# The first transfer of `p` moved from SyncE's transfer queue to ScalarE's, in a fused attention and token-mixing kernel

## The chip, the cores and the metric

The kernel runs on one core of one Trainium2 chip. A core has a matrix engine (TensorE, PE in the profile), three engines for element-wise work (VectorE, DVE; ScalarE, ACT; GpSimd, POOL) and SyncE (SP), which does no arithmetic. Each engine works through its own instruction list in order and waits on semaphores where it needs another's result. Data come from and go to device memory (HBM) through 16 DMA engines, which the five instruction lists feed: a transfer issued by SP or ACT stands in the profile as `hardware_dynamic`, one issued by POOL as `software_dynamic`. The metric is the device time of the kernel in microseconds; lower is better.

## The reference

Two attention steps and a token-mixing step, over a batch of 8, with 8 heads, 576 tokens and 64 channels a head; `p` holds 32 packing queries for each head. Cut to what matters:

```python
p_packed = sm_attn(p, k, v)               # softmax(p k^T / 8) v : 32 x 64 for each head
out = sm_attn(q, p_packed, p_packed)      # softmax(q p_packed^T / 8) p_packed : 576 x 64 for each head
x = out.transpose(0, 2, 1, 3).reshape(8, 576, 512)
wq, wk = x @ w_q, x @ w_k                 # 576 x 64
W_tok = einsum('bsd,btd->bst', wq, wk) / 8
mixed = einsum('bst,btd->bsd', W_tok, x)
result = maximum(mixed, 0) @ w_out        # float32, 8 x 576 x 512
```

## The kernel before

The work is cut by batch element; the 8 batches run as a software pipeline, so that stages of several batches stand interleaved. The order is written out by hand: one string, `SCHEDULE`, lists some 600 small operations as `name@batch`, then a letter for the engine that copies a result (`s` ScalarE, `v` VectorE, `g` GpSimd) and the accumulator banks. A loop at the end of the kernel (L796 to L802) emits them in that order. Each engine's instruction list is what this string gives that engine, and no scheduler changes it.

For one batch: `k` (transposed per head by TensorE, `kt`, and copied to `kT`, `ke`) meets `p` in `s0` (L345); `nm0`, `ex0` and `ex1` make the exponentials; `xt` transposes them; `pv` (L421) multiplies by `v`; `pp`, `pt`, `pq` give the packed values and their products with the weights; `q` is transposed (`qt`), scored against the packed values (`e0` to `e2`, L470 and L482), and the later names up to `o0` to `o4` (L755) are the mixing and the last product, whose results SyncE stores.

Loads. Most go out on GpSimd's queue, because they turn float32 in HBM into bfloat16 on chip: `LK`, `LQ`, `LV` (`load`, L146 to L155) bring a whole batch of `k`, `q` or `v`, 576 KB as written on chip and twice that as read. `PB` (L178) brings all of `p` in bfloat16, `cw0` to `cw3` and `wo0`, `wo1` the weights. Batch 0 is treated apart, so that the pipeline fills sooner:

- `PF` (L164 to L166) loads `p` of batch 0 in float32 into `p_f`, 64 KB; `pfc@0s` (L213) casts it to `p_h` on ScalarE; `tp` (L217) transposes it on TensorE, and `lp` copies it to `pT_bd`, which `s0` reads.
- `KB` and `KA` (`first_k`, L168) load `k` of batch 0 in float32 on SyncE's queue in two halves of 576 KB, `kf[1]` first. `cB0`, `cB1`, `cA0` (VectorE) and `cA1` (ScalarE) cast them to `k_sb` (L247); `kf2`, `kf3` transpose the half of `KB`, `kf0`, `kf1` that of `KA` (L252), and `kfe0` to `kfe3` copy the results to `kT`.
- `w1` and `w2` (L200) are matrix products of a zero tile, with no use for the result.

The start of the order reads:

```python
SCHEDULE = """
    w1@0c:6 LQ@0 PF@0 pfc@0s KB@0 cw3@0 w1@0f:1 cB1@0v w1@0f:2 w2@0f:1 cw0@0 PB@0 LV@0 cB0@0v LK@1
    w1@0c:2 LK@2 KA@0 id@0 w1@0f:2 cA1@0s w1@0c:6 LQ@1 w2@0c:1 w1@0c:6 w2@0f:0 w1@0c:7 tp@0:0
    kf3@0:1 w1@0f:5 kf2@0:5 w1@0c:3 LV@1 cA0@0v kfe3@0v kf1@0:7 cw2@0 kf0@0:4 lp@0v w1@0f:6 w1@0c:0
```

Read by engine, SyncE's list begins `PF`, `KB`, `KA`, and its next entry is a store of results. GpSimd's begins `LQ@0`, `cw3`, `cw0`, `PB`, `LV@0`, `LK@1`, `LK@2`, `id` (the identity matrix for the transposes), `LQ@1`, `LV@1`. ScalarE's begins with the load of its function table, then `pfc`, `cA1`. The ninth transfer of GpSimd's list, `LV@1`, waits for the first to land, and so on.

Of the kernel before, what the change touches and what calls it, by code (L numbers as in the profile page):

```python
# [68 lines left out]
def kernel(  # L69
# [12 lines left out]
    nc = tc.nc  # L82
# [77 lines left out]
    p_f = sbp.tile([P, 2, Dh], fp32, name="p_f")  # L160
# [2 lines left out]

    @op  # L164
    def PF(b):
        nc.sync.dma_start(p_f, p[0].rearrange("(g x) l d -> (x l) g d", g=2))  # L166

    def first_k(gp, b):  # L168
        nc.sync.dma_start(
# [663 lines left out]
```

## Time and profile before

| | us |
|---|---|
| median of 3 runs | 119.72 |
| lowest, highest | 119.58, 120.13 |
| the profiled execution's own time | 119.49 |
| its span, first to last instruction | 117.7 |

| engine | busy us | share of the span |
|---|---|---|
| TensorE, products | 105.6 | 90% |
| VectorE | 91.1 | 77% |
| ScalarE | 88.0 | 75% |
| GpSimd | 60.1 | 51% |

The profile is of one execution, whose time is 0.23 us under the median of the runs; what lies outside its span is 119.49 - 117.7 = 1.8 us. Times within it are counted from the span's start. In the rows, `SPq` and `POOLq` (or POOL with `DMA_DIRECT2D`) are the issuing of a transfer; a row's brackets give the idle time of the engine before it and what ended it. `x20` is the number of instructions merged into a row, and rows of one engine may overlap. GB/s counts the bytes as written, so a load that halves the width reads twice its figure. A DMA share is a sum of the times of packets over 16 engines; as packets of one engine overlap, it can be over 1.

### The profile page before, as it was taken

How to read it: one execution, taken by the hardware profiler on the slowest of the kernel's cores; microseconds unless marked ns; L12 is line 12 of the kernel's file. 1: busy time of each engine (PE TensorE's matmuls, PEld its weight loads, DVE VectorE, ACT ScalarE, POOL GpSimd, SP SyncE). 2: the span in 40 equal slices, each digit the busy share in tenths (PEclk: the TensorE clock that was granted, in tenths of full speed). 3: DMA queues.
4: the chain of work that ended last, by engine and by line, in shares of the span. 5: the costliest groups of instructions: out<-in, count | busy, mean ns of one | idle time of the engine just before them, and what ended most of it. 6: DMA issues, size and time to landing. Idle time of an engine off the chain costs nothing.

```text
span 117.7 us, 4778 instructions
## 1 busy us (share of the span) xinstructions
PE 105.6 (90%) x2065; PEld 68.6 (58%) x2081; DVE 91.1 (77%) x184; ACT 88.0 (75%) x164; POOL 60.1 (51%) x88
## 2 busy tenths in 40 slices
PE   5997587887988999999999999999999999999950
PEld 1234456575855857778665875867566566545520
DVE  5326958999989989999999999698999967571420
ACT  5005574699879899899589999999898967678430
POOL 6965342278558994645981283606697780000000
PEclk9999999999999999999999999999999999999997
DMA  3999999999999999999999999999932174464793
GB/s 41 291 269 198 213 202 207 208 198 208 208 208 206 207 207 209 209 207 208 251 249 207 207 207 282 220 205 362 354 138 89 57 305 166 199 267 184 288 369 145
DMA packets 17925, 25.47 MB, mean 216 GB/s; under 512 B 2160, under 2 KB 14448, under 8 KB 17904
## 3 DMA queue, kind: packets, MB, share of 16 engines
q0 software_dynamic: 13920, 14.49, 73.2%
q1 hardware_dynamic: 3984, 10.68, 24.0%
q8 instruction: 16, 0.26, 0.8%
q14 instruction: 5, 0.04, 0.1%
HBM read 30.21 MB, written 9.44 MB: 337 GB/s over the span
## 4 chain that ended last, share of the span: by engine, by line
PE 63%; DMA 23%; DVE 7%; issue 2%; POOL 2%; ACT 1%; DVEq 0%; POOLq 0%
PE psum L755 27%; DMA k_sb<-in_k_dram 16%; PE psum L304 8%; DMA q_sb<-in_q_dram 7%; PE psum L421 3%; PE psum L714 3%; PE psum L571 3%; PE psum L660 3%; PE psum L376 3%; PE psum L628 2%; PE psum L470 2%; PE psum L345 2%; PE psum L683 1%; DVE nmax L355 1%; DVE kT L141 1%
## 5 line engine op out<-in xcount | busy, mean ns | idle before, releaser
L755 PE MATMUL psum<-w_out,r 128*64 128x512 bf16 (+1 forms) x208 | 30.9, 380 | 0.6 <-issue 0.3
L551 POOL TENSOR_TENSOR a<-e,rr 128x512 bf16<-128x512 f32 (+1 forms) x19 | 16.6, 891 | 7.2 <-ACT e L135 2.5
L755 PEld LDWEIGHTS <-r 128*64 128x64 bf16 (+1 forms) x216 | 12.3, 108 | 10.2 <-issue 1.1
L135 ACT ACTIVATE o_sb<-psum 128x512 f32<-128x512 f32 x24 | 14.5, 609 | 4.2 <-PE psum L755 4.2
L135 ACT ACTIVATE r<-psum 128x512 bf16<-128x512 f32 x24 | 13.3, 603 | 1.9 <-PE psum L714 1.9
L203 PE MATMUL psum<-zero 128*64 128x512 bf16 (+1 forms) x43 | 11.9, 487 | 2.5 <-DVE zero L182 1.2
L498 DVE TENSOR_REDUCE mx<-psum 128x16 f32<-128x512 f32 (+1 forms) x24 | 12.5, 551 | 1.8 <-PE psum L470 1.6
L359 ACT ACTIVATE e1T<-psum,nmax 128x576 bf16<-128x576 f32 x16 | 11.8, 740 | 2.8 <-DVE nmax L355 2.6
L502 DVE TENSOR_TENSOR e<-psum,mx 128x512 f32<-128x512 f32 (+1 forms) x24 | 12.4, 549 | 0.3
L540 POOL TENSOR_TENSOR rt<-e 128x576 f32<-128x576 f32 x5 | 7.1, 1422 | 10.3 <-ACT e L531 10.3
L355 DVE TENSOR_REDUCE nmax<-psum 128x2 f32<-128x1152 f32 x8 | 10.8, 1354 | 0.9 <-PE psum L345 0.8
L304 PE MATMUL psum<-ident,q_sb 128*64 128x128 bf16 x288 | 10.2, 220 | 0.4 <-DMA q_sb<-in_q_dram 0.4
L531 ACT ACTIVATE e<-e 128x1152 f32<-128x1152 f32 x8 | 9.3, 1164 | 1.0 <-DVE e L502 1.0
L135 ACT ACTIVATE kT<-psum 128x1280 bf16<-128x1280 bf16 (+3 forms) x8 | 8.0, 1013 | 2.3 <-PE psum L304 2.3
L304 PEld LDWEIGHTS <-q_sb 128*64 128x64 bf16 x288 | 8.6, 110 | 1.0 <-DMA q_sb<-in_q_dram 0.5
L304 PE MATMUL psum<-ident,k_sb 128*64 128x128 bf16 x252 | 9.0, 220 | 0.1
L141 DVE COPY o_sb<-psum 128x512 f32<-128x512 f32 x8 | 5.5, 685 | 4.0 <-PE psum L755 3.8
L542 POOL TENSOR_TENSOR rt<-rt 128x288 f32<-128x288 f32 (+2 forms) x15 | 7.9, 527 | 1.2
L148 POOL DMA_DIRECT2D v_sb<-in_v_dram x8 | 6.2, 779 | 4.3 <-DMA q_sb<-in_q_dram 2.4
L304 PEld LDWEIGHTS <-k_sb 128*64 128x64 bf16 x252 | 7.8, 110 | 0.9 <-issue 0.2
L203 PEld LDWEIGHTS <-zero 128*64 128x64 bf16 (+1 forms) x50 | 3.7, 116 | 7.9 <-issue 6.0
L135 ACT ACTIVATE qT<-psum 128x1024 bf16<-128x1024 bf16 (+1 forms) x7 | 7.5, 1092 | 0.6 <-PE psum L304 0.6
(95 smaller groups left out, 227.9 us busy)
## 6 DMA issues: line engine op xcount, KB each, us to landing
out_dram<-o_sb SPq DMA_DIRECT2D x14, 512.0 KB, 3.7
q_sb<-in_q_dram POOLq DMA_DIRECT2D x8, 576.0 KB, 17.2
v_sb<-in_v_dram POOLq DMA_DIRECT2D x8, 576.0 KB, 17.1
k_sb<-in_k_dram POOLq DMA_DIRECT2D x7, 576.0 KB, 18.4
k_f<-in_k_dram SPq DMA_DIRECT2D x2, 576.0 KB, 5.6
out_dram<-ox SPq DMA_DIRECT2D x4, 256.0 KB, 3.8
out_dram<-o_sb SPq DMA_DIRECT2D x4, 256.0 KB, 2.5
w_out<-in_moe_w_out_dram POOLq DMA_DIRECT2D x2, 256.0 KB, 14.9
```

The lines of the kernel that those rows point to most:

```text
L135: nc.scalar.activation(dst, src, func, scale=scale)
L203: nc.tensor.matmul(bank(ks[0])[r], zero[:, r], zero, start=True, stop=True, skip_group_check=True,)
L304: nc.tensor.transpose(tp[64 * g2:64 * g2 + 64, gp, :, 64 * (j - j0):64 * (j - j0) + 64], S_[b][src][:, gp + 2 * g2, order[j]], ident,)
L355: nc.vector.tensor_reduce(tile("nmax", [P, 2], fp32, b), S_[b]["s1"], axis=AX, op=MAX, negate=True)
L359: nc.scalar.activation(tile("e1T", [P, NJ, 2, 64], bf16, b)[:, :, h2], S_[b]["s1"][:, h2].rearrange("a (j s) -> a j s", j=NJ), EXP, bias=S ...
L498: nc.vector.tensor_reduce(units(i, tile("mx", [P, NU, 1], fp32, b)), S_[b]["e", i], axis=AX, op=MAX)
L502: nc.vector.tensor_tensor(units(i, tile("e2", [P, NU, L], fp32, b)), S_[b]["e", i], m.to_broadcast((P, m.shape[1], L)), op=SUB,)
L531: nc.scalar.activation(e, e, EXP, scale=scale)
L540: nc.gpsimd.tensor_tensor(t, e[:, :, 0:16], e[:, :, 16:32], op=ADD)
L542: nc.gpsimd.tensor_tensor(t[:, :, 0:w], t[:, :, 0:w], t[:, :, w:2 * w], op=ADD)
L551: (nc.gpsimd if on == "g" else nc.vector).tensor_tensor(tile("a2", [P, NU, L], bf16, b)[:, r], S_[b]["e2"][:, r], S_[b]["rr"][:, r].to_bro ...
L755: nc.tensor.matmul(ps[r], src[:, i, r], w_out[:, i, :], start=(i == 0), stop=(i == 3),)
```

## The change

`PF` is issued from ScalarE instead of SyncE. Nothing else is changed, and the schedule string stays as it was: since `PF` stands before `pfc` in it, the transfer becomes the first instruction of ScalarE's list, ahead of the load of its function table, and SyncE's list begins with `KB`. The lists of TensorE, VectorE and GpSimd, and all waits, are the same in both kernels; `pfc` waits for the same transfer.

```diff
     @op
     def PF(b):
-        nc.sync.dma_start(p_f, p[0].rearrange("(g x) l d -> (x l) g d", g=2))
+        nc.scalar.dma_start(p_f, p[0].rearrange("(g x) l d -> (x l) g d", g=2))
```

## The prediction

> **What bounds the kernel now.** I read the page first: the span, the slices and the chain that ended last.
>
> ```profile
> span 117.7 us, 4778 instructions
> ...
> PE   5997587887988999999999999999999999999950
> ...
> DMA  3999999999999999999999999999932174464793
> ...
> PE 63%; DMA 23%; DVE 7%; issue 2%; POOL 2%; ACT 1%; DVEq 0%; POOLq 0%
> ```
>
> A slice is 2.94 us. The DMA engines are full from the second slice to the twenty-ninth, and TensorE only from the fourteenth. So two things bound the span in turn: transfers at first, then TensorE. The chain in order of time says where the one hands over to the other.
>
> ```profile
> 0.64 0.62 issue
> 1.25 8.57 DMA q_sb<-in_q_dram
> ...
> 10.11 0.74 POOL v_sb L148
> 10.85 1.21 POOL wqk L278 x2
> 12.06 18.39 DMA k_sb<-in_k_dram
> 30.49 0.75 PE psum L304 x20
> ```
>
> The start of the chain is the landing of the first `q`, and then a load of `k` issued at 12.06 that lands 18.39 us later, at 30.45. From 30.49 on it is engines, above all TensorE. The reader should see that the wait is not for one slow transfer: that load stands behind those issued before it in GpSimd's queue. Whatever lets this queue begin to drain sooner brings all of its landings forward, as long as the queue never runs empty. Its rate in the stretch, from the windows view (after the stretch and its length come busy time and instructions of PE, PEld, DVE, ACT and POOL; at the end TensorE's clock, the DMA share and GB/s):
>
> ```profile
> 1.80:2.40 0.60, 0.60 (x4) 0.24 (x3) 0.55 (x2) 0.22 (x1) 0.60 (x2) 1.00 0.60 121
> 2.40:3.40 1.00, 1.00 (x3) 0.15 (x1) 0.72 (x5) 0.31 (x1) 1.00 (x2) 1.00 0.71 81
> 3.40:4.40 1.00, 1.00 (x4) 0.23 (x3) 0.33 (x2) 0.00 (x0) 1.00 (x3) 1.00 1.03 389
> ...
> 5.00:8.00 3.00, 3.00 (x21) 0.94 (x17) 1.12 (x2) 0.00 (x0) 2.67 (x5) 1.00 1.11 287
> ...
> 10.00:18.00 8.00, 5.91 (x145) 4.20 (x143) 5.36 (x12) 4.90 (x12) 4.09 (x6) 1.00 1.20 208
> 18.00:30.00 12.00, 10.05 (x240) 7.62 (x240) 11.03 (x20) 8.96 (x15) 6.59 (x9) 1.00 1.25 205
> ```
>
> From 10 to 30 us a steady 205 to 208 GB/s is written, which for loads that halve the width is about 413 GB/s read: this is the bound of the first quarter of the span. Only at 2.4 to 3.4 us do the engines carry little (81 GB/s). TensorE, for its part, is short of data in the same stretch:
>
> ```profile
> 9.61 0.69 PE L257 MATMUL psum<-ident,k_sb 128*64 128x128 bf16 x18 [0.58 <-ACT k_sb L135]
> 10.55 0.41 PE L203 MATMUL psum<-zero 128*64 128x512 bf16 x2 [0.25 <-issue]
> 10.89 0.68 PE L345 MATMUL psum<-kT,pT_bd 128*64 128x512 bf16 x8
> ...
> 24.14 0.75 PE L304 MATMUL psum<-ident,q_sb 128*64 128x128 bf16 x20 [0.38 <-DMA q_sb<-in_q_dram]
> ...
> 26.87 0.70 PE L421 MATMUL psum<-v_sb,e 64*64 64x128 bf16 x36 [0.23 <-DMA v_sb<-in_v_dram]
> ```
>
> It waits at 9.61 for the second half of the first `k`, and at 24.14 and 26.87 for landings of GpSimd's queue.
>
> **The change part by part.** It takes one issue out of SyncE's list and puts one at the head of ScalarE's. The timeline of the start:
>
> ```profile
> 0.74 1.28 ACT L135 ACT_TABLE_LOAD   x1 [0.74 <-PEq L817]
> 0.74 0.45 SPq L166 DMA_DIRECT2D p_f<-in_p_dram  x1
> ...
> 1.25 0.96 SPq L169 DMA_DIRECT2D k_f<-in_k_dram  x2
> 1.25 0.93 POOL L148 DMA_DIRECT2D q_sb<-in_q_dram  x1 [0.81 <-POOLq L817]
> ...
> 2.72 0.31 ACT L135 ACTIVATE p_h<-p_f 128x128 bf16<-128x128 f32 x1 [0.70 <-DMA p_f<-in_p_dram]
> ...
> 5.40 1.12 DVE L141 CAST k_sb<-k_f 128x512 bf16<-128x512 f32 x2 [1.54 <-DMA k_f<-in_k_dram]
> ...
> 7.52 0.23 PE L219 MATMUL psum<-ident,p_h 128*128 128x128 bf16 x1
> ...
> 8.93 0.63 ACT L135 ACTIVATE k_sb<-k_f 128x512 bf16<-128x512 f32 x1 [5.90 <-DMA k_f<-in_k_dram]
> ```
>
> *ScalarE.* One more issue, 0.45 us by SyncE's row, then the table load, now 1.19 to 2.47 instead of 0.74 to 2.02. The cast of `p_f` starts at 2.72 now, so even a later table load ends before it. Behind the cast, ScalarE idles 5.90 us until 8.93, and TensorE wants `p_h` only at 7.52, after its zero products. The cover for a late `p_f` is 7.52 - 0.31 - 2.72 = 4.5 us; the row charged is therefore 0.
>
> *SyncE.* `KB` is issued at 0.74 instead of 1.25, and `KA` after it: 0.51 us sooner. Does the data follow the issue, or does it follow the end of `p_f`? The DMA view of 1.8 to 2.4 us, in 40 steps of 0.015 us, tells:
>
> ```profile
> GB/s 0 0 51 68 102 102 137 102 102 137 188 239 222 205 222 222 205 205 188 154 120 154 119 119 154 103 86 119 137 86 69 69 34 34 34 34 171 17 17 307
> DMA packets 275, 0.07 MB, mean 121 GB/s; under 512 B 272, under 2 KB 272, under 8 KB 275
> ```
>
> Small packets of `p_f` begin in the third step, at 1.83, 0.64 us after the end of their issue (0.74 + 0.45 = 1.19). The first large packets, of `KB`, stand at the right end, from step 37, at 2.34; half of the `k_f` row is an issue, so the first ended at 1.25 + 0.48 = 1.73, and 0.61 us passed. The two delays are alike, so the `k` data follow their own issue and would start at about 1.83. The end of `p_f` is at the same place, so the row cannot exclude that the ring, not the issue, set it; both vanish with the change.
>
> *What 0.51 us is worth.* By the windows, once running, the queue of `k` alone carries 389 GB/s (3.4 to 4.4). GpSimd's data do not start until shortly after that: the DMA view of 3.4 to 4.4 has one queue, that of 5 to 8 has both.
>
> ```profile
> DMA packets 169, 0.39 MB, mean 389 GB/s; under 512 B 0, under 2 KB 0, under 8 KB 169
> ## 3 DMA queue, kind: packets, MB, share of 16 engines
> q1 hardware_dynamic: 169, 0.39, 103.0%
> ```
>
> ```profile
> q0 software_dynamic: 257, 0.30, 57.0%
> q1 hardware_dynamic: 249, 0.56, 54.5%
> ```
>
> So by the time GpSimd's data set in, `k` is ahead by 0.51 x 389 = 198 KB. In the shared stretch its queue moves 0.56 MB in 3 us, 187 GB/s, so the second half would land 198/187 = 1.06 us sooner, at about 7.9 instead of 8.93. TensorE can use of this only its idle time of 0.58 at 9.61, since zero products and the transposes of the first half fill it until 9.03; the chain of `s0`, the exponentials and `pv` that follows moves by that at most. GpSimd's queue has the engines to itself sooner, and at 413 GB/s read the 198 KB are worth 0.48 us: all its landings, among them those at 24.14, 26.87 and 30.49, come 0.48 us sooner, as a full queue has no gap to swallow it. The smaller of the two, 0.48, passes on; from 30.49 TensorE and VectorE follow one another, and the tail shifts as a block.
>
> *What `p_f` takes back.* Its 64 KB no longer come before `k` but beside it. If they fall into the thin stretch (81 GB/s at 2.4 to 3.4), they cost 0; if into full flow, 64/389 = 0.17 us. I take 0, because its row's data begin at 1.83, well before the full flow. Bounds of the whole step: from 0.48 - 0.17 = 0.31 to the full 0.51 us.
>
> The Trainium skill (DMA: Bandwidth & Descriptors, "Issuing engines are not separate DMA queues") speaks against more: all issuing engines share the same 16 DMA engines, and issuing from several at once saves only the sequencer's time. By it the gain is capped at the removed issue, 0.51 us, and the third rival below gets little; no run here shows it yet.
>
> Sum against the profiled execution: 119.49 - 0.48 = 119.01. The median of the runs lies 0.23 above it, so 119.72 - 0.48 = 119.24 is what I give, rounded to 119.2. A change under 0.5%, 0.6 us, is about what a measurement of this kernel can't tell from none; the bound on the fast side is 119.12, so this forecast lies close to it.
>
> **The rivals.** *(1) No change.* The thin stretch ends at a fixed time, near 3.4 us, whatever was issued when, because something else of the start (VectorE's fills, GpSimd's first issues) holds the engines. Then the earlier issue only waits longer, the landings stay, and the time is 119.7. For it: 81 GB/s though two transfers were queued. Against it: `p_f` just before ran at 121 GB/s in packets of 256 bytes, and what slows the large packets starts with them.
>
> *(2) Slower: `p_f` starves.* Two hardware queues compete, and the small packets of `p_f` wait behind the large ones of `k`. It decides once `p_f` lands later than 7.52 - 0.31 = 7.21; if it lands only with the second half of `k`, at 8.93, then `p_h` is ready at 9.24, the transpose starts 1.72 us later, and the 1.51 us of TensorE work between 7.52 and 9.03 puts the next transposes at 10.75 instead of 9.61, 1.14 us late. The waits for landings at 24.14 and 26.87 could swallow 0.61 of it. So 120.25 to 120.86, say 120.6. For it: nothing in the trace has both hardware queues at work. Against it: in 5 to 8 us two queues had 257 and 249 packets, a fair share; sharing in turn, 16 packets a DMA engine are through with some 16 of `k`. The Trainium skill (DMA: Bandwidth & Descriptors, "Queues, rings and completion order") says that each DMA engine takes turns between its queues; the 257 to 249 agree.
>
> *(3) Faster than the sum.* The thin stretch is caused by `p_f` and `k` being in one ring (its completion writes, or the second issue behind it). Apart, `k` flows fully from its start, and of the 1.00 us at 81 GB/s a share of 1 - 81/389 = 0.79 us is won on top: 119.24 - 0.79 = 118.45. TensorE's idle 0.58 and 0.25 before `s0` would limit its side to 0.83, and the later landings carry the rest, so 118.4 to 118.9. For it: the stretch follows directly on `p_f`. Against it: `p_f` was done when it began.
>
> **How the numbers follow.** The forecast 0.60, rival 1 0.10, rival 2 0.15 (the trace has no transfer on ScalarE's queue that would speak against it outright), rival 3 0.15. The runs of before scatter by 0.55 us, and 119.24 is 0.12 above the bound, so a little under half of the forecast's chance, 0.27, falls on faster: faster 0.27 + 0.15 = 0.42, same 0.33 + 0.10 = 0.43, slower 0.15. Its own range is 119.0 to 119.5 (0.31 to 0.51 us, and scatter). The range for 8 in 10 takes in most of rival 3 and rival 1 and leaves out rival 2: 118.5 to 120.0.
>
> **What would show it.** Right: `KB`'s issue at 0.74 and its first large packets near 1.83; the cast of `k_f` on ScalarE near 7.9; TensorE's idle time before L257 gone; the landing of the first `q` near 9.3 and the TensorE row now at 30.49 near 30.0, with the same distance from there to the end. Wrong: large packets that begin at 1.83 but a flow of 389 GB/s that starts at 3.4 as now (rival 1), or at 2.0 (rival 3); a `p_h` row after 7.2 and a TensorE wait on it (rival 2). If the row at 30.49 moves but the end does not, an engine's own work after it is the bound, and my step from landing to end is the one that failed.

## The result, and the profile after

The changed kernel takes 118.97 us (median of 8 runs, 118.54 to 119.29) against 119.70 (8 runs, 119.51 to 120.13): a ratio of 0.9936 with a 95% interval of 0.9916 to 0.9956. Two later series gave 0.9947 (0.9923 to 0.9970) and 0.9945 (0.9922 to 0.9968). It is faster by 0.5 to 0.6%, some 0.6 to 0.7 us. The ratios, but not the medians, leave out runs over 1.5% above the fastest of the same kernel; that matters below for two orders of which a part of the runs lies there.

The page of the profiled execution (its own time 119.11 us), with the same lines as before:

```profile
span 117.3 us, 4794 instructions
...
PE   5999788898988999999989999999999999999960
...
DMA  3999999999999999999999999999832174464793
...
q0 software_dynamic: 13920, 14.49, 73.5%
q1 hardware_dynamic: 3712, 10.62, 23.6%
...
q10 hardware_dynamic: 272, 0.07, 0.2%
...
PE 48%; DMA 38%; POOL 8%; issue 2%; ACT 1%; POOLq 0%
```

There is a queue that did not exist before, q10, with the 272 packets of `p`. TensorE's slices near the start are fuller (the first seven read 5999788 instead of 5997587). The timeline of the start, with the rows that answer to those before:

```profile
0.74 0.47 ACTq L166 DMA_DIRECT2D p_f<-in_p_dram  x1
0.74 0.96 SPq L169 DMA_DIRECT2D k_f<-in_k_dram  x2
...
1.24 1.28 ACT L135 ACT_TABLE_LOAD   x1 [1.24 <-PEq L817]
...
5.38 1.13 DVE L141 CAST k_sb<-k_f 128x512 bf16<-128x512 f32 x2 [1.51 <-DMA k_f<-in_k_dram]
...
5.60 0.31 ACT L135 ACTIVATE p_h<-p_f 128x128 bf16<-128x128 f32 x1 [3.08 <-DMA p_f<-in_p_dram]
...
6.99 0.63 ACT L135 ACTIVATE k_sb<-k_f 128x512 bf16<-128x512 f32 x1 [1.08 <-DMA k_f<-in_k_dram]
...
7.30 0.23 PE L219 MATMUL psum<-ident,p_h 128*128 128x128 bf16 x1
...
8.65 0.67 PE L257 MATMUL psum<-ident,k_sb 128*64 128x128 bf16 x18
...
9.90 0.68 PE L345 MATMUL psum<-kT,pT_bd 128*64 128x512 bf16 x8
```

`k` is issued 0.51 us sooner, as the change says. Three things differ from a plain shift by that amount. `p`, issued at 0.74 as ever, is cast at 5.60 instead of 2.72. The first half of `k` is cast at 5.38, where it was at 5.40: no gain at all. The second half is cast at 6.99 instead of 8.93, 1.94 us sooner, and `s0` starts at 9.90 instead of 10.89. The windows and the DMA views show what happened on the way (columns as before):

```profile
1.80:2.40 0.60, 0.60 (x4) 0.24 (x3) 0.55 (x2) 0.60 (x1) 0.60 (x2) 1.00 0.99 88
2.40:3.40 1.00, 1.00 (x3) 0.15 (x1) 0.72 (x5) 0.12 (x1) 1.00 (x3) 1.00 0.69 237
3.40:4.40 1.00, 1.00 (x4) 0.23 (x3) 0.33 (x2) 0.00 (x0) 1.00 (x3) 1.00 0.91 331
```

The next rows are of the DMA view of 1.8 to 2.4 us, in steps of 0.015 us, and of 3.4 to 4.4 us:

```profile
GB/s 0 0 307 154 154 0 154 154 154 154 154 0 0 307 0 307 0 154 154 0 154 0 0 154 154 0 0 0 0 154 0 154 0 0 0 154 154 154 0 0
DMA packets 23, 0.05 MB, mean 88 GB/s; under 512 B 0, under 2 KB 0, under 8 KB 23
...
q1 hardware_dynamic: 133, 0.29, 74.2%
q10 hardware_dynamic: 153, 0.04, 16.7%
```

The large packets of `k` begin in the third step, at 1.83, where `p` began before. The thin stretch moved with them: 88 GB/s at 1.8 to 2.4, and 237 at 2.4 to 3.4 where it was 81. Of `p` there is no packet up to 2.4 (none under 512 bytes); most of them, 153, fall into 3.4 to 4.4, among 133 of `k` at full flow. The rest of the answer is who came next. From 4.7 to 5.4 us the DMA view of the kernel before has GpSimd's queue at work, that of the changed kernel has not:

```profile
q0 software_dynamic: 81, 0.09, 77.1%
q1 hardware_dynamic: 45, 0.09, 36.3%
```

```profile
q1 hardware_dynamic: 125, 0.28, 101.7%
q10 hardware_dynamic: 19, 0.00, 2.8%
```

So the second half of `k` had the engines nearly to itself in that stretch, 0.28 MB instead of 0.09, and the first `q` on GpSimd's queue waited. Which is why the second half of `k` won 1.94 us and the first `q` only 0.22, as the chain of waits shows:

```profile
1.24 8.36 DMA q_sb<-in_q_dram
...
9.89 0.74 POOL v_sb L148
10.63 1.21 POOL wqk L278 x2
11.84 17.84 DMA k_sb<-in_k_dram
29.72 0.75 PE psum L304 x20
...
41.09 18.02 DMA v_sb<-in_v_dram
59.16 0.70 PE psum L421 x36
...
112.98 0.60 ACT o_sb L135
```

The load of `k` that TensorE waits for lands at 29.68 instead of 30.45, and TensorE goes on at 29.72 instead of 30.49, 0.77 us sooner. The last piece of TensorE's and ScalarE's work, though, comes 0.42 sooner (112.98; 113.40 before). The chain names what lies between: at 59.16 a product waits for `v` of batch 4, which before it did not.

How much sooner GpSimd's queue drains can be counted: the DMA view of the first 24 us gives its packets. Before:

```profile
q0 software_dynamic: 3620, 3.61, 90.3%
```

After:

```profile
q0 software_dynamic: 3689, 3.69, 92.3%
```

That is 69 packets more. In the microsecond from 23 to 24 it moves 180 in the kernel before, so it is 69/180 = 0.38 us ahead.

### The profile page after: what moved, and what is told of

Same layout as the page of the kernel before. It is cut to its first block, busy times and chain, and to the rows that moved or that the text cites. A ratio compares the mean times of both kernels' runs of the same rounds, so it can differ in the third digit from the quotient of the medians.

```text
span 117.3 us, 4794 instructions
## 1 busy us (share of the span) xinstructions
PE 107.4 (92%) x2081; PEld 68.6 (58%) x2081; DVE 91.3 (78%) x184; ACT 88.3 (75%) x164; POOL 60.2 (51%) x88
## 4 chain that ended last, share of the span: by engine, by line
PE 48%; DMA 38%; POOL 8%; issue 2%; ACT 1%; POOLq 0%
PE psum L755 23%; DMA v_sb<-in_v_dram 15%; DMA k_sb<-in_k_dram 15%; DMA q_sb<-in_q_dram 7%; PE psum L304 4%; PE psum L714 3%; PE psum L660 2%; PE psum L571 2%; PE psum L421 2%; PE psum L470 2%; PE psum L376 2%; POOL a L551 2%; PE psum L628 2%; POOL rt L542 1%; POOL rt L540 1%
## 5 line engine op out<-in xcount | busy, mean ns | idle before, releaser
L755 PE MATMUL psum<-w_out,r 128*64 128x512 bf16 (+1 forms) x216 | 31.7, 380 | 0.0
L203 PE MATMUL psum<-zero 128*64 128x512 bf16 (+1 forms) x50 | 13.9, 466 | 1.7 <-DVE zero L182 1.2
L141 DVE COPY kT<-psum 128x1024 bf16<-128x1024 bf16 (+3 forms) x10 | 6.9, 690 | 1.6 <-PE psum L257 1.1
```

The costliest lines, as they stand in the source:

```text
L141: nc.vector.tensor_copy(dst, src)
L203: nc.tensor.matmul(bank(ks[0])[r], zero[:, r], zero, start=True, stop=True, skip_group_check=True,)
L755: nc.tensor.matmul(ps[r], src[:, i, r], w_out[:, i, :], start=(i == 0), stop=(i == 3),)
```

## The experiments

Each kernel was timed beside the kernel before on the same chip; the medians of the latter lay at 119.54 to 119.70. The table gives the median of all runs and the ratio to the kernel before. The last six columns are of one profiled execution each: its own time, starts in us from the timeline, and packets from the DMA view.

| kernel | median us | ratio, 95% interval | profiled run, us | second half of k cast | `s0` | row of 30.49 | last o_sb copy | q0 packets by 24 us |
|---|---|---|---|---|---|---|---|---|
| before | 119.70 | | 119.49 | 8.93 | 10.89 | 30.49 | 113.40 | 3620 |
| after | 118.97 | 0.9936 (0.9916 to 0.9956) | 119.11 | 6.99 | 9.90 | 29.72 | 112.98 | 3689 |
| again | 118.92 | 0.9947 (0.9923 to 0.9970) | 118.97 | 6.79 | 9.64 | 29.96 | 112.87 | 3689 |
| again2 | 118.96 | 0.9945 (0.9922 to 0.9968) | 119.39 | 7.39 | 9.73 | 29.76 | 113.26 | 3694 |
| both | 119.85 | 1.0023 (0.9989 to 1.0056) | 119.45 | 9.29 | 11.25 | 30.51 | 113.42 | 3588 |
| late_p | 118.75 | 0.9933 (0.9910 to 0.9956) | 118.67 | 6.46 | 9.75 | 29.68 | 112.58 | 3730 |
| k_p_k2 | 119.59 | 0.9968 (0.9939 to 0.9996) | 119.85 | 9.80 | 11.76 | 30.87 | 113.76 | 3629 |
| k_k_p2 | 119.92 | 1.0004 (0.9976 to 1.0033) | 119.18 | 6.24 (VectorE's part) | 11.06 | 30.17 | 113.07 | 3703 |
| split | 118.94 | 0.9940 (0.9919 to 0.9960) | 119.46 | 7.17 | 9.92 | 30.37 | 113.35 | 3676 |
| split2 | 118.92 | 0.9936 (0.9917 to 0.9955) | 119.22 | 7.09 | 10.24 | 30.20 | 113.12 | 3675 |
| after_half | 118.86 | 0.9943 (0.9923 to 0.9963) | 118.86 | 6.66 | 9.95 | 29.86 | 112.75 | 3703 |
| before_half | 119.56 | 0.9998 (0.9976 to 1.0020) | 119.58 | 9.03 | 11.00 | 30.55 | 113.45 | 3622 |

The first series of the two orders `k_p_k` and `k_k_p` are given in the text; their profiles are of executions of 122.25 and 121.55 us.

**The changed kernel again.** No edit.

> The changed kernel once more, unaltered. Theory: the gain is real and of the size of the drain of GpSimd's queue plus what TensorE still wins after it, so a ratio of 0.992 to 0.997 and a profile with the first float32 p cast near 5.6, the second half of the first k near 7.0 and the wait for the load of v at 59. Rival: the profiled loss of 0.35 between 30 and 59 us was an accident of that one execution; then this profile keeps 0.8 to 1.0 of lead to the end and has no wait at 59.

> The changed kernel once more, beside the next three on the same chip. Both theories: ratio 0.992 to 0.997; it is the yardstick.

The gain is there twice more. In the profile of the first, TensorE's row is at 29.96 and the end 0.53 us sooner than before, just as much as the row: the tail moved as a block, with no wait at 59. Neither forecast of `again` holds whole: the wait is absent, as the rival has it, but the lead is 0.53 and not 0.8 to 1.0. In the second there is a wait, and the end kept only 0.14 of 0.73:

```profile
59.44 0.70 PE L421 MATMUL psum<-v_sb,e 64*64 64x128 bf16 x36 [0.73 <-DMA v_sb<-in_v_dram]
```

So the loss at 59 belongs to single executions, and a profile that has it (119.11 and 119.39 us) is of a slower run than one that has not (118.97).

**Is the wait at 59 a bound?** A load ahead of that `v` in GpSimd's queue is halved, in the changed kernel and in the one before: half of `k` of batch 6 is left out, so the output of these two kernels is not the reference's.

```diff
         t = tile(name, [P, 4, NJ, Dh], bf16, b)
+        n = 2 if (name, b) == ("k_sb", 6) else 4
         nc.gpsimd.dma_start(
-            t.rearrange("p g j d -> p g (j d)"),
-            src[b].rearrange("(g h2) (sp j) d -> (h2 sp) g (j d)", h2=2, j=NJ),
+            t.rearrange("p g j d -> p g (j d)")[:, 0:n],
+            src[b].rearrange("(g h2) (sp j) d -> (h2 sp) g (j d)", h2=2, j=NJ)[:, 0:n],
         )
```

> The changed kernel with half of the load of k of batch 6 left out (its output is not the reference's), which frees the queue of 288 KB, about 1.4 us, ahead of the load of v of batch 4. Theory (TensorE's lead of 0.77 at 30 us is cut to 0.42 at 59 by the landing of that v): the wait at 59 goes, and 0.3 to 0.4 us more are won, about 118.6. Rival (the lead is lost on TensorE or VectorE): no change against the changed kernel, 119.0.

> The kernel before with the same half load of k of batch 6 left out. Theory (there TensorE reaches the product with v of batch 4 just as it lands, so the queue did not hold it): 119.6 to 119.8, no change. Rival (the queue binds the kernel before too): 119.3 or less.

My expectation for the changed kernel failed: 118.86 against 118.92 for the changed kernel beside it, where 118.6 was expected. The wait at 59 is absent from its profile, as from that of `again`, and the median gained nothing by that: the typical run was not held by it. The control did not move (0.9998).

**Which part of the change is it?** Here `p` keeps its new queue, but `k` its old time: the same transfer goes out once more at the head of SyncE's list.

```diff
     def PF(b):
+        nc.sync.dma_start(p_x, p[0].rearrange("(g x) l d -> (x l) g d", g=2))
         nc.scalar.dma_start(p_f, p[0].rearrange("(g x) l d -> (x l) g d", g=2))
```

> p goes out twice: on ScalarE's queue as in the changed kernel, and once more, into a tile that nobody reads, at the head of SyncE's queue, so that k is issued at 1.25 as before. Theory (the 0.51 us of earlier issue is the cause): no gain, 119.7 to 119.9, the extra 64 KB costing up to 0.17. Rival (p on a queue of its own is the cause, whenever k starts): 118.9 to 119.2, and the second half of k still lands near 7 to 7.5.

The theory holds: 119.85, no gain, and TensorE's row stands at 30.51. The extra 64 KB are in that time too, but the price that the expectation gives them, up to 0.17, could not hide a gain of 0.6 to 0.7. The queue for `p` alone is worth nothing. GpSimd's data again begin before 5 us; from 4.7 to 5.4 its queue has these packets:

```profile
q0 software_dynamic: 71, 0.08, 76.3%
q1 hardware_dynamic: 35, 0.07, 29.6%
```

**Earlier `k`, without ScalarE's queue.** Two orders on SyncE's list alone, made by the schedule string of the kernel before (its lines are cut on the right):

```diff
-    w1@0c:6 LQ@0 PF@0 pfc@0s KB@0 cw3@0 w1@0f:1
+    w1@0c:6 LQ@0 KB@0 PF@0 pfc@0s cw3@0 w1@0f:1
```

```diff
-    w1@0c:6 LQ@0 PF@0 pfc@0s KB@0 cw3@0 w1@0f:1
-    w1@0c:2 LK@2 KA@0 id@0
+    w1@0c:6 LQ@0 KB@0 KA@0 PF@0 pfc@0s cw3@0 w1@0f:1
+    w1@0c:2 LK@2 id@0
```

The first, `k`, `p`, `k`:

> All three first transfers on SyncE's queue, in the order first half of k, p, second half of k; ScalarE issues none. Theory (the 0.51 us of earlier issue of k is the cause, not whose queue p is on): 118.9 to 119.2, the TensorE row of 30.49 near 30.0. Rival (p needs a queue of its own): 119.5 to 119.8. Side question: GpSimd's data began when the first two transfers of SyncE's queue were through, in all six profiles so far; if that holds, they begin near 4.5 here, the second half of k shares the engines again, and it lands at 8.3 to 9.0, not near 7.0.

> The order first half of k, p, second half of k on SyncE's queue once more, since the profiled execution of the first look had one DMA engine end its share of the second half at 10.96 where the others ended by 8.13. Theory (the earlier issue is what counts): a median within 0.2 of the changed kernel's, and in a usual execution the second half of k lands at 8.3 to 9.0. Rival (a queue for p is worth something of its own): 0.3 to 0.5 above the changed kernel.

It gave 0.9963 (0.9939 to 0.9987) and 0.9968 (0.9939 to 0.9996), with medians of 119.08 and 119.59: faster than before, but not steadily. Of the 13 runs of the first series one lies at 122.25 and the rest between 118.75 and 120.38; of the 12 of the second 7 lie between 118.94 and 119.85 and 5 between 121.76 and 122.93. The 7 have a median of 119.13, 0.17 above the changed kernel beside it, which is the theory's (within 0.2); only the median of all 12 would speak for the rival. By the ratios the gain is 0.3 to 0.4%, against 0.5 to 0.6% for the changed kernel, with intervals that overlap, so that it is smaller is not shown. What the order does is seen in a profile of 119.85 us; none of a run near 119.1 was taken. The second half of `k` is third in its queue here, shares the engines with GpSimd's data from before 4.7 us on, and is cast at 9.80, later than expected and later than before the change:

```profile
9.80 0.63 ACT L135 ACTIVATE k_sb<-k_f 128x512 bf16<-128x512 f32 x1 [4.20 <-DMA k_f<-in_k_dram]
...
10.48 0.69 PE L257 MATMUL psum<-ident,k_sb 128*64 128x128 bf16 x18 [1.84 <-ACT k_sb L135]
...
30.87 0.73 PE L304 MATMUL psum<-ident,k_sb 128*64 128x128 bf16 x20
```

TensorE waits 1.84 us, and in this execution nothing is left of the lead. In the other profile, of an execution of 122.25 us, the same cast stands at 11.29, behind 17 packets of the second half that trickle in from 8.2 to 11.0 us; whether that is behind all the runs near 122 was not tried. So `k` gains by its earlier issue without ScalarE's queue; what the queue adds is that `p` no longer stands between the halves, and in these two profiles the second half landed late behind it.

The second, `k`, `k`, `p`:

> All three on SyncE's queue, both halves of k first, p last. Theory: k gains its 0.51 us, but p lands behind it, after 7.0; the cast of p then ends after 7.2 and TensorE waits for it, 0.2 to 1.0 us on its own side; as the landing near 30 us still comes 0.4 earlier, 119.0 to 119.4. Rival (p is never late enough to matter): 118.9 to 119.1, with no wait of TensorE before the transpose of p.

> Both halves of k, then p, on SyncE's queue once more, for a second profile. Theory (p comes behind k and then shares with GpSimd's data, lands after 7.2, and TensorE waits for it): a wait of 1 to 2.5 us ahead of the transpose of p, p cast at 8 to 9.3, and 119.4 to 120.2. Rival (the first profile was an accident): p cast before 7.2 and 118.9 to 119.1.

This is the slower rival of the prediction, and the theory's wait is there. `p` is cast at 8.09, past the point of 7.21 (in the profile of the first series, of 121.55 us, at 9.08, and TensorE waits 2.13 us):

```profile
8.09 0.31 ACT L135 ACTIVATE p_h<-p_f 128x128 bf16<-128x128 f32 x1 [6.07 <-DMA p_f<-in_p_dram]
...
8.46 0.23 PE L219 MATMUL psum<-ident,p_h 128*128 128x128 bf16 x1 [1.77 <-ACT p_h L135]
```

GpSimd's queue is ahead by 83 packets (3703 against 3620), more than in the changed kernel, and yet the time is 0.9996 (0.9978 to 1.0015) and 1.0004 of that before, with medians of 119.97, above the 119.0 to 119.4 expected, and 119.92, as expected. The profiled execution, 119.18 us, is one of the fastest of its series and still ends 0.33 us sooner than before; that in the typical run the queue's lead and TensorE's wait cancel out is argued from the ratios, and no trace shows it. Compare the columns of `s0` and of the row of 30.49 in the table: here and in `k_p_k2` they are 19.11 us apart, in all others of the table more. In these two, no wait of TensorE for a landing stands between them, so 19.11 is taken as its own way; where the distance is longer, it waited for landings (in the kernel before at 24.14 and 26.87). In the kernel before it is 19.60, in the changed one 19.82. So TensorE could have been at the row 0.5 and 0.7 us sooner: the landing, not the start of `s0`, sets the tail in both.

**Does `p`'s early issue matter?** A small ScalarE copy stands ahead of the transfer.

```diff
     def PF(b):
+        nc.scalar.activation(p_x, zero[:, 0:128].rearrange("p (g d) -> p g d", g=2), COPY)
         nc.scalar.dma_start(p_f, p[0].rearrange("(g x) l d -> (x l) g d", g=2))
```

> The changed kernel with one small ScalarE operation (a copy of zeros into a tile that nobody reads) ahead of the transfer of p, so that ScalarE's table load comes first and p is issued some 1.6 us later, near 2.3. Theory (p has 4.5 us of cover and only k's issue counts): as the changed kernel within 0.2, p cast between 5.6 and 7.2. Rival (the early issue of p on ScalarE has a part in the gain): 0.3 or more above the changed kernel.

`p` was issued only 0.44 us later, at 1.18, since ScalarE's queue went on beside the table load; the 1.6 us of the expectation did not come about, and the test is weaker for it. The outcome is the theory's: 118.75, 0.21 under the changed kernel beside it, with intervals that overlap (0.9910 to 0.9956 against 0.9922 to 0.9968). That it is the better of the two is not shown, but its profile has the largest lead: 3730 packets by 24 us, 110 more than before, 0.61 us, and `p` is cast at 4.90, sooner than in the changed kernel (5.60) though issued later.

**Both queues for `k`.** The second half goes out on ScalarE's queue, `p` behind the first half on SyncE's (`split`) or ahead of the second on ScalarE's (`split2`). The string's order is changed to match; the line common to both:

```diff
     def first_k(gp, b):
-        nc.sync.dma_start(
+        (nc.scalar if gp == 0 else nc.sync).dma_start(
```

> The first half of k on SyncE's queue and the second on ScalarE's, both issued at 0.74; p after the first half, on SyncE's. Theory (what counts is when the engines begin to carry k at the full rate): the start is the changed kernel's, 1.83, so no more than that kernel's gain, 118.8 to 119.2. Rival (the thin second after k's start is a delay of each queue, and two queues pass it together): up to 0.4 us more, 118.5.

> p, then the second half of k on ScalarE's queue; the first half of k on SyncE's. Theory: as the changed kernel, 118.8 to 119.2; p lands sooner than 5.4. Rival (two queues pass the thin second together): about 118.5.

Both are as fast as the changed kernel, 118.94 and 118.92, and not faster: that two queues pass the thin stretch together and win 0.4 us is not borne out. `p` is cast at 6.95 in `split`, where TensorE waits 0.74 us for it, and at 5.62 in `split2`, where it was to land before 5.4.

## Why the prediction was right, and where its sizes were off

The time given was 119.2 (119.24 by the sum) and 118.97 came; the sign, the cause and the wide range were right. The gain, 0.48 us in the sum, was 0.6 to 0.7, and the three medians of the changed kernel, 118.97, 118.92 and 118.96, lie just under the forecast's own range of 119.0 to 119.5. Whether the gain could be told from none was left about even (0.42 against 0.43).

*The data follow the issue.* Right: `k` begins at 1.83, 0.51 us sooner, and where it does not (`both`) there is no gain. The Trainium skill (DMA: Bandwidth & Descriptors, "Issuing engines are not separate DMA queues") has issuing from two engines save the sequencer's time only; the trace agrees, as what `k` won at its start is the 0.51 us of one issue. The cap of 0.51 us on the whole gain, which the prediction drew from it, is not borne out by the medians; two of the three intervals include it.

*The thin stretch.* Rival 1 tied it to a fixed time and rival 3 to `p` in the same ring. Both fall: it moved with `k`, and in the changed kernel, with `p` in another ring, it is still there (88 GB/s at 1.8 to 2.4).

*`p` costs nothing.* This is the step that failed in its reason. I let its 64 KB fall into the thin stretch; most of its packets, 153 of 272, fell into 3.4 to 4.4, behind it, about one for one with those of `k` (133). The first half of `k` lost all of its 0.51 us by that: it is cast at 5.38, but at 4.77 in `k_k_p2`, where `p` comes after `k`. For the queue's lead, the prediction had 0.48 us, or 0.31 if `p` met the full flow; 0.38 to 0.41 was counted, between the two. With `p` 0.44 us later it was 0.61, more than the issue gave; why is open.

*ScalarE's cover.* It was needed. I charged nothing for a late `p` because 4.5 us lay behind it; `p` came 2.88 us later than before and in one repeat 3.32 (cast at 6.04). Rival 2 was therefore closer than its chance of 0.15 suggests, and `k_k_p` and `k_k_p2` show its price: the ratio is back at 1 (the rival's own figure was 120.25 to 120.86).

*The second half of `k`.* Mis-sized: 7.9 was given, 6.99 measured. I had GpSimd's data begin at the same time and share the engines; they began after 5.4. On TensorE's side 0.58 us was taken as the limit, and `s0` moved by 0.99: 0.22 of it because the zero products ended sooner (the transpose of `p` at 7.30 instead of 7.52), which the prediction took as fixed. They vary from one execution to the next: the transpose stands at 7.05 and 7.14 in the two repeats, and at 7.05 in `before_half` as well, where `k` has its old time. The rest of the 0.99, 0.19, fits the idle 0.25 at 10.55, which is gone. Neither size changed the result, since the landing near 30 us was the later of the two, as the 19.11 us show.

*The landing.* It was to move from 30.49 to 30.0; it moved to 29.72, 29.96 and 29.76 in three profiles, by 0.53 to 0.77. This is where the sum was too small. The queue as a whole was 0.38 to 0.41 us ahead; how that lead spread over the single loads was not measured, so the 0.15 to 0.39 us between the two stay open. The first `q`, which was to land near 9.3, landed at 9.60, 0.22 sooner than before.

*The tail as a block.* It held: in every profile without a wait at 59 the last copy and the row of 30.49 moved by the same amount within 0.07 us (late_p 0.82 and 0.81, again 0.53 and 0.53, k_p_k2 0.36 and 0.38 later). In the two with it, the step from landing to end lost 0.35 and 0.59. So the 0.42 us by which the end moved in the first profile are near the 0.48 of the sum by luck: 0.77 was won at the landing and 0.35 lost at 59.

## What to carry to other kernels

The first transfer of a kernel that is bound by its transfers is worth its issue time, so let the queue begin with what everything waits for, and put what has slack elsewhere; but work out how late the moved one may land, since it may lose more than the other gains (2.88 us against 0.51 here). Ask what stands second and third in the queue too: the same earlier start was worth 0.5 to 0.6% with `p` out of the way, about nothing with `p` behind `k`, and 0.3 to 0.4%, less steadily, with `p` between its halves. And judge a shift at a late landing over several profiles, as one execution can lose it to a wait that the next does not have.

## What was not expected of the hardware

GpSimd's data began by what stood at the head of SyncE's queue. Its first packet came between 4.1 and 4.6 us where these were `p` and half of `k` in either order (before, `before_half`, `both`, `k_p_k`, `k_p_k2`), and between 5.2 and 5.7 us where they were both halves of `k`; in either case the first two transfers were then nearly through. But with half of `k` on each queue it came at 5.7 (`split`) and 5.8 (`split2`), and in `split2` SyncE's queue has only one transfer, so these two are not the whole rule. The profile of `k_k_p2` has just the first of them in 4.7 to 5.4 us:

```profile
q1 hardware_dynamic: 126, 0.28, 100.2%
q0 software_dynamic: 7, 0.01, 6.6%
```

GpSimd's issue stood at 1.25 in all of them. The Trainium skill (DMA: Bandwidth & Descriptors, "Queues, rings and completion order") has each DMA engine take turns between its queues by packets; the two hardware queues agree (153 and 133 packets in 3.4 to 4.4), while GpSimd's first load begins later than its turn would come, if it was ready by then, which no view shows. Why was not tried.

Two transfers issued at 0.74 from two engines did not begin together: `k` at 1.83, `p` at 2.9, though before, alone at the head of a queue, it needed 0.64 us from the end of its issue. ScalarE's queue is not late by itself: in `both`, where `p` heads both queues, it starts at 2.0, and the DMA view of 1.8 to 2.4 us has most of its packets:

```profile
q1 hardware_dynamic: 274, 0.07, 54.6%
q10 hardware_dynamic: 239, 0.06, 44.1%
```

In `split` the half of `k` at the head of ScalarE's queue starts only at 2.7. So what came late was what was issued beside a `k` at the head of SyncE's queue; why was not tried.
